# A long convolution with a gated MLP: second rows transposed by a DMA, eleven up products copied out by ScalarE, the first units fed tile by tile, and a new order of tasks

## The chip, the cores and the metric

The kernel runs on one core of a Trainium2 chip. The metric is the device time of one execution in microseconds (us). Shown for the kernel before are the median of three runs and one profiled execution with its trace. Engines are named as in the profile: PE (TensorE matmul), PEld (its weight loads), DVE (VectorE), ACT (ScalarE), POOL (GpSimd) and SP (SyncE, which here only issues DMAs).

## The reference, cut to what matters

The sequence has S = 2048 rows, the model D = 512 columns, the MLP Df = 1792. `A_q` is the row input x; all inputs and the output are bf16.

```python
def _A_ref(q, k, v, shift_k, ssm_k, ssm_D):
    ...
    for t in range(ks):
        k_shift = k_shift + k_pad[:, t:t + S, :] * shift_k[:, ks - 1 - t][None, None, :]
    kv = k_shift * v
    L = 2 * S
    ...
    y_f = kv_f * kf_f[None, :, :, :]
    y = irfft2(y_f, s=(1, L)).astype(jnp.bfloat16)[:, 0, :S, :]
    y = y + kv * ssm_D[None, None, :]
    return q * y

def _B_ref(x, w_gate, w_up, w_down):
    g = jnp.einsum("bsd,df->bsf", x, w_gate)
    u = jnp.einsum("bsd,df->bsf", x, w_up)
    h = _gelu(g) * u
    return jnp.einsum("bsf,fd->bsd", h, w_down)

x = A_q
xn = _layernorm(x, axis=-1)
s = _A_ref(xn, A_k, A_v, A_shift_k, A_ssm_k, A_ssm_D)
g = _silu(_B_ref(xn, B_w_gate, B_w_up, B_w_down))
return x + s * g
```

So there are two independent halves that meet at the end: a causal convolution of length 2048 along the rows (by transforms of length 4096), and a gated MLP on the normalised rows.

## The kernel before, in words

**Layernorm and transposition.** The rows are 16 tiles of 128. Statistics (L837, L838), variance (L848), the power -1/2 on GpSimd (L850) and the normalisation (L858 on ACT, L859 on DVE) make XN from X. The MLP works on row groups q = 0 to 3 of four tiles. For each the transposed rows, xnT, are needed as an operand; xnT has two buffers, used by q in turn. In `xn_transpose` the groups q = 0 and 1 are transposed on PE (L880, four transposes for each tile) and brought from PSUM to xnT by ACT (L621) or DVE (L624); the groups q = 2 and 3 are transposed by one DMA each, issued by SP (L872).

**Units.** A unit (q, m) is one group of 512 rows against one chunk m (0 to 13) of 128 MLP columns: four gate matmuls and four up matmuls (L630, one for each 128 columns of D), a gelu of the gate on ACT into GE (L1183, three buffers), and on DVE the product of GE with the up result, read from PSUM, into HT (L1186). The first two units of q = 0 (`N_HALF`) are cut into two halves of 256 rows, each with its own gelu and product (L1174, L1176). After the units of a group come its `down` matmuls: for each row tile 14 matmuls over the chunks (L630, HT and Wd), then a tanh and a product into G (L1210, L1212), or for the last group a silu, the product with XN and the addition of X (L1218, L1220, L1221). The last row tile is cut into 384 and 128 columns.

**The convolution.** The kernel taps Hn are transposed on PE (L904) into HTr. Stage 1 (`stage1`) then runs on the taps ("H", L946) and on the product of the shifted k with v ("K", L938; the shift is L995 to L1003 on DVE). It has eight units for each. An H unit is four matmuls of 64 rows, two evictions of 1024 columns by ACT (L621) into a slot, an addition on DVE (L955), and a store of the slot to DRAM (`ZH`, 512 KB, a DMA on the ACT queue). The H slots are four, and lie in the late halves of X and XN, which the trace therefore names as the destination; a slot can be taken again only when its store has landed, and the late rows of x can be loaded there only after that. The K units store to `ZK` on the SP queue. Later stages read ZH and ZK back (L1018 and others), multiply the spectra (L1121), go back by way of `ZI`, and give y (L1256), from which the output is formed (L1265 to L1285).

**The order.** Every task (some matmuls, one eviction, one DMA) is added to a list `S` with its possible engines and its estimated cost. `SEQ` is one sequence of task numbers that was found before by a search; a number with a `b` takes the task's second engine. `Sched.run` walks `SEQ`, assigns pool buffers and emits the tasks in that order, so each engine gets its instructions in a fixed order, and a recording layer puts in the semaphore waits. Each engine and each DMA queue works in order: what stands behind a waiting instruction waits too. The planner's costs don't change a kernel by themselves; they decide how buffers are handed out, and were what the search for `SEQ` used. PSUM has eight banks, shared by units, stage 1 and the rest.

**Loads.** All the loads stand on the SP queue in the order of `ORDER`: x, the taps, the weights in chunks, k and v last. Behind the last load of v (SP's row of two V loads at 34.42) come the small transposes of tables (L1029) and the `ZK` stores.

Of the kernel before, what the change touches and what calls it, by code (L numbers as in the profile page):

```python
# [6 lines left out]
BF16 = mybir.dt.bfloat16  # L7
# [46 lines left out]
NC_PAIRS = 4  # L54
SMALL = 1.15 * 262144
T_FWD = 219.0
N_HALF = 2


class Res:  # L60
# [345 lines left out]
def build_kernel(nc, A_q, A_k, A_v, A_shift_k, A_ssm_k, A_ssm_D, B_w_gate, B_w_up, B_w_down, out):  # L406
    with ExitStack() as es0:
# [39 lines left out]
        Drow = new("Drow", [1, DM], BF16)  # L447
        xnT_at = place["at"] + 4096
        xnT = new("xnT", [128, 2, 4, KD, 128], BF16)
        GE = new("GE", [128, 3, 512], BF16)  # L450
        ast_at = place["at"]
        AST = new("AST", [128, 2, 2, 2, DM], BF16)
        g_at = place["at"]
# [889 lines left out]
```

## Time and profile before

| what | value |
|---|---|
| median of three runs | 191.09 us (190.99 to 191.48) |
| the profiled execution, its time | 190.94 us |
| the profiled execution, its span | 189.1 us |
| ACT's share of the span | 72% |
| transposes of XN on PE | 32, of 128 columns each |
| DMA issues of the ZH stores | 8 of 512 KB, all from the ACT queue |

The span runs from the first instruction to the last that the profile shows; 1.84 us of the execution's own time lie around it. A line of the profile reads: source line, engine, operation, destination and source by the program's names, partitions x elements, type, how many, then busy time, mean time of one, and the idle time of the engine just before with what ended it. A timeline line begins with start and length in us; a matmul's end is modelled, so for a run of matmuls the distance between starts is its price. In a DMA issue the last number is the time from the issue to the landing. Names such as "X" and "XN" stand also for the stage-1 slots in their late halves.

### The profile page before, as it was taken

The numbers are of one execution on the slowest core, as the hardware profiler recorded it, in microseconds if no ns is written. First come the engines' busy times: TensorE is split into PE (matmuls) and PEld (weight loads), VectorE is DVE, ScalarE is ACT, GpSimd is POOL, SyncE is SP. The second block draws the span as 40 slices with busy tenths as digits, with TensorE's granted clock in tenths as the row PEclk, the third lists the DMA queues.
The fourth block names the chain that finished last, engine by engine and source line by source line (L and its number), as shares of the span: only waits on it lengthen the run. The fifth ranks groups of instructions, "written<-read, shape, count | busy, mean of one in ns | idle before, by whom it ended". The sixth has DMA issues, their size and how long they took to land.

```text
span 189.1 us, 3534 instructions
## 1 busy us (share of the span) xinstructions
PE 183.5 (97%) x1386; PEld 78.4 (41%) x1386; DVE 168.4 (89%) x250; ACT 136.1 (72%) x185; POOL 12.7 (7%) x26
## 2 busy tenths in 40 slices
PE   7889999999999999999999999999999999999993
PEld 2566344343344333334443433433343444443442
DVE  6979999999999999997499988989999994569994
ACT  6388988996766877876867699887997851253651
POOL 5310920000000000022000000000000000000000
PEclk9999999999999999999999999999999999999999
DMA  5999999999769668289997763999523353967335
GB/s 178 326 382 337 339 373 373 401 414 275 304 239 272 208 227 334 111 243 327 224 310 231 245 206 104 392 284 372 188 112 114 111 170 100 386 208 244 110 142 198
DMA packets 36422, 47.84 MB, mean 253 GB/s; under 512 B 7347, under 2 KB 26039, under 8 KB 36406
## 3 DMA queue, kind: packets, MB, share of 16 engines
q1 hardware_dynamic: 29878, 39.23, 63.7%
q10 hardware_dynamic: 6528, 8.39, 12.5%
q8 instruction: 11, 0.18, 0.4%
q14 instruction: 5, 0.04, 0.1%
HBM read 27.39 MB, written 14.68 MB: 222 GB/s over the span
## 4 chain that ended last, share of the span: by engine, by line
PE 92%; DVE 3%; ACT 2%; POOL 1%; issue 0%
PE psall L630 78%; PE psall L1018 6%; PE psall L946 2%; PE psall L938 2%; PE psall L1256 2%; PE psall L904 2%; POOL mv L850 1%; PE psall L880 1%; ACT L737 1%; DVE stats L837 1%; DVE XN L859 0%; DVE G L1221 0%; DVE G L1220 0%; DVE C L709 0%; ACT G L1218 0%
## 5 line engine op out<-in xcount | busy, mean ns | idle before, releaser
L630 PE MATMUL psall<-xnT,Wu 128*128 128x512 bf16 (+1 forms) x232 | 56.2, 372 | 0.0
L630 PE MATMUL psall<-xnT,Wg 128*128 128x512 bf16 (+1 forms) x232 | 55.3, 372 | 0.5 <-DVE xnT L624 0.5
L630 PE MATMUL psall<-Wd,HT 128*128 128x512 bf16 (+2 forms) x238 | 51.6, 367 | 0.0
L1186 DVE TENSOR_TENSOR HT<-psall,GE 128x512 bf16<-128x512 f32 x54 | 36.1, 680 | 6.5 <-PE psall L630 6.2
L1183 ACT ACTIVATE GE<-psall 128x512 bf16<-128x512 f32 x54 | 31.4, 600 | 12.9 <-PE psall L630 11.6
L630 PEld LDWEIGHTS psall<-Wd,HT 128*128 128x128 bf16 x238 | 21.7, 98 | 27.0 <-issue 3.6
L630 PEld LDWEIGHTS psall<-xnT,Wg 128*128 128x128 bf16 x232 | 21.1, 98 | 27.9 <-issue 3.6
L630 PEld LDWEIGHTS psall<-xnT,Wu 128*128 128x128 bf16 x232 | 21.6, 98 | 26.4 <-issue 2.3
L621 ACT ACTIVATE BO<-psall 128x1024 bf16<-128x1024 f32 x19 | 19.0, 1023 | 7.7 <-PE psall L1018 4.0
L1121 DVE TENSOR_TENSOR HSW<-KB,HSW 128x2048 bf16<-128x2048 bf16 x16 | 19.3, 1220 | 0.3 <-ACT KB L621 0.2
L621 ACT ACTIVATE HSW<-psall 128x1024 bf16<-128x1024 f32 x16 | 15.8, 1031 | 3.5 <-PE psall L1018 3.5
L621 ACT ACTIVATE KB<-psall 128x1024 bf16<-128x1024 f32 x14 | 13.9, 1022 | 2.1 <-PE psall L1018 1.9
L999 DVE TENSOR_TENSOR KTM<-KK,SKB 128x2048 bf16<-128x2048 bf16 x12 | 14.5, 1208 | 0.1
L1001 DVE TENSOR_TENSOR KAC<-KAC,KTM 128x2048 bf16<-128x2048 bf16 x12 | 14.5, 1207 | 0.1
L621 ACT ACTIVATE AST<-psall 128x1024 bf16<-128x1024 f32 x12 | 12.3, 1023 | 1.4 <-PE psall L938 1.2
L1210 ACT ACTIVATE G<-psall 128x512 bf16<-128x512 f32 x12 | 7.2, 601 | 7.8 <-PE psall L630 6.8
L850 POOL TENSOR_TENSOR mv<-mv,NHALF 128x1 f32<-128x1 f32 (+1 forms) x7 | 7.1, 1021 | 67.4 <-DVE mv L848 64.7
L837 DVE BATCH_NORM_STATS2 stats<-X 128x6 f32<-128x512 bf16 x16 | 10.8, 683 | 0.8 <-DMA X<-in_A_q_dram 0.8
L1121 DVE TENSOR_TENSOR KB<-KB,HSW 128x2048 bf16<-128x2048 bf16 x8 | 9.6, 1222 | 0.1
L1144 DVE TENSOR_TENSOR HSW<-HSW 128x2048 bf16<-128x2048 bf16 x8 | 9.7, 1218 | 0.0
L621 ACT ACTIVATE X<-psall 128x1024 bf16<-128x1024 f32 x8 | 8.2, 1023 | 1.0 <-PE psall L946 0.9
L621 ACT ACTIVATE XN<-psall 128x1024 bf16<-128x1024 f32 x8 | 8.1, 1024 | 1.0 <-PE psall L946 0.9
(85 smaller groups left out, 152.3 us busy)
## 6 DMA issues: line engine op xcount, KB each, us to landing
BH<-ZH SPq DMA_DIRECT2D x8, 512.0 KB, 4.4
BK<-ZK SPq DMA_DIRECT2D x8, 512.0 KB, 6.3
HSW<-HSW SPq DMA_DIRECT2D x16, 256.0 KB, 3.5
ZI<-BO ACTq DMA_DIRECT2D x16, 256.0 KB, 3.0
BI<-ZI SPq DMA_DIRECT2D x8, 512.0 KB, 4.7
ZK<-AST SPq DMA_DIRECT2D x6, 512.0 KB, 3.1
Hn<-in_A_ssm_k_dram SPq DMA_DIRECT2D x4, 512.0 KB, 7.4
KK<-in_A_k_dram SPq DMA_DIRECT2D x4, 512.0 KB, 11.2
```

The lines of the kernel that those rows point to most:

```text
L621: return h.activation(o, i, ACTF.Copy, scale=scale)
L630: return h.matmul(o, lhsT=l, rhs=r, start=st, stop=sp)
L837: t_stats[t] = op([("DVE", 670.0)], lambda e, h, t=t: h.bn_stats(stats[:, t, :], X[:, t, :]), r=[bX[q][t % 4]], w=[bst[t]], rr=[R_X[t]], w ...
L850: t_pw = op([("POOL", 2500.0 if q else 600.0)], lambda e, hd, ts=ts, n=n: hd.tensor_tensor(mv[:, ts, 3:4], mv[:, ts, 2:3], NHALF[:, 0:n, : ...
L999: op([("DVE", dur)], lambda e, h, j=j, m=m: h.tensor_tensor(KTM[:, m.slot, :, :], kk(j), sk(j), ALU.mult), r=need + [bSKB[j], a], w=[m], r ...
L1001: op([("DVE", dur)], lambda e, h, m=m: h.tensor_tensor(KAC[:, a.slot, :, :], KAC[:, a.slot, :, :], KTM[:, m.slot, :, :], ALU.add), r=[m], ...
L1018: trk.op("PE", lambda h: h.matmul(ps(s, i)[b, :], lhsT=wt(col)[a, :], rhs=data(col)[a, :], start=n < 16, stop=n >= len(todo) - 16, tile_po ...
L1121: return hd.tensor_tensor(pair(KB, *(2 * DM * z for z in slots())) if to else x, k, x, ALU.mult)
L1144: return hd.tensor_tensor(x, x, y, ALU.add)
L1183: op([("ACT", act(512))], lambda e, h: h.activation(GE[:, g.slot, :], bank(pg), ACTF.Gelu_apprx_tanh), r=[pg], w=[g], rr=lambda: R_bank(pg ...
L1186: op([("DVE", dve(512, 1))], lambda e, h: h.tensor_tensor(HT[:, q % 2, m, :], bank(pu), GE[:, g.slot, :], ALU.mult), r=[pu, g], w=[bHT[q][m]],
L1210: op([("ACT", act(n))], lambda e, h, g=g, pc=pc: h.activation(g, pc(), ACTF.Tanh, scale=0.5), r=[p], w=[bt], rr=lambda p=p: R_bank(p), ww= ...
```

## The change

The change has five parts.

1. `xn_transpose`: the second row group (q = 1) is transposed by a DMA on SP too, without a condition on earlier units. Its 16 PE transposes and four evictions go.
2. `UNITS`: for 11 units, (0, 6), (0, 8), (0, 10), (0, 12) and (1, 0) to (1, 12) with even m, the up result is first copied from PSUM into a new bf16 buffer `U_` of two slots, and the product is taken from there. In the built program all eleven copies stand on ACT.
3. The first two units of q = 0: the gate and up matmuls go by single row tiles (64 matmuls of 128 columns in the place of 32 of 256). Their gelus and products stay as they were.
4. The variance of the layernorm (`var`) takes the transform table `F1` as a further input of its task; and the planner's costs for the SP queue's DMAs are others (a transposition's 6700 becomes 4300, its landing is computed anew).
5. `SEQ` is a new sequence. Seen on the engines: the eight H units of stage 1 stand ahead of the first unit of q = 1, as do 42 of the 56 down matmuls of q = 0 (before: seven H units and nine down matmuls). On ACT the first four ZH stores stand in one group behind the last gelus of q = 0, and the four others follow one by one. The last y group (L1256) has 38 down matmuls behind it where it had 42. The four evictions of xnT of q = 0 are on ACT (two were on DVE). In the first microseconds the sine table and its load come later on ACT and the iotas for the identities earlier on GpSimd. The new DMA stands on SP behind the last load of v and ahead of the small transposes.

```diff
@@ -25,27 +25,28 @@
 SEQ = (
-    "2 3 16 0 7 17 18 19 20 21 1 10 8 22 9 11 23 24 25 65 66 12 4 6 48 67 26 5 73b 49 68 76 74 75 86 90 77 78 87 71 91b 27 28 29 30 72 82 83 69 70 "
...
+    "16 17 18 19 2 4 6 3 0 20 21 7 10 11 22 1 8 9 23 24 25 65 66 5 73b 67 12 68 76 74 75 77 69 49 86 90 48 78 361 26 70 27 79b 28 87 349 91 71 351 72 "
...
 )
@@ -55,6 +56,7 @@
 N_HALF = 2
+UNITS = [(0, 6), (0, 8), (0, 10), (0, 12), (1, 0), (1, 2), (1, 4), (1, 6), (1, 8), (1, 10), (1, 12)]
@@ -372,7 +374,13 @@
-                if en < self.EARLY:
+                if eng == "SP":
+                    pipe = max(pipe, t.start + 780.0, max(l.end for l in order if l.eng == "loads") - 760.0) + t.nbytes / self.DMA_BW
+                    t.end = pipe + 760.0
+                    if t.nbytes > 750000.0 and t.start < 52000.0:
+                        t.end = max(t.end, t.start + 9700.0)
+                        pipe = t.end - 760.0
+                elif en < self.EARLY:
@@ -448,6 +456,7 @@
+        U_ = new("U_", [128, 2, 512], BF16)
@@ -537,6 +546,7 @@
+        R_U = [res(f"U{j}", U_[:, j, :]) for j in range(2)]
@@ -575,6 +585,7 @@
+        pU = Pool_("U", 2)
@@ -846,7 +857,7 @@
-                t_var = op([("DVE", 180.0)] + ([] if q else [("ACT", 240.0)]), var, r=[bconst, *bm], w=[be], rr=rm + [R_ep], ww=rm)
+                t_var = op([("DVE", 180.0)] + ([] if q else [("ACT", 240.0)]), var, r=[bconst, bF1, *bm], w=[be], rr=rm + [R_ep], ww=rm)
@@ -866,11 +877,11 @@
         def xn_transpose(q):
-            if q > 1:
+            if q > 0:
...
-                S.add([("SP", 6700.0)], f, r=bXN[4 * q:4 * q + 4], w=bxnT[q], nbytes=W_XT, after=gu_tasks[q - 2])
+                S.add([("SP", 4300.0)], f, r=bXN[4 * q:4 * q + 4], w=bxnT[q], nbytes=W_XT, after=gu_tasks[q - 2] if q > 1 else [])
                 return
@@ -1170,7 +1181,8 @@
                     for p, W, nm in ((p2[0], Wg, "g"), (p2[1], Wu, "u")):
-                        gu_tasks[q].append(S.add([("PE", pe(4, 256))], half(p, W, nm, 2 * i, 2 * i + 2), r=[bW[nm][ci], *bxnT[q][2 * i:2 * i + 2]], w=[p], lat=150.0))
+                        for j in (2 * i, 2 * i + 1):
+                            gu_tasks[q].append(S.add([("PE", pe(4, 128))], half(p, W, nm, j, j + 1), r=[bW[nm][ci], bxnT[q][j]], w=[p], lat=150.0))
@@ -1183,6 +1195,12 @@
             af = (down_tasks[q - 2] if q >= 2 else []) + (s1_tasks["H"] if q == 1 else [])
+            if (q, m) in UNITS:
+                ub = B(f"ub{q}_{m}", pU)
+                op(EV(512), lambda e, h: copy(e, h, U_[:, ub.slot, :], bank(pu)), r=[pu], w=[ub], rr=lambda: R_bank(pu), ww=lambda: [R_U[ub.slot]])
+                op([("DVE", dve(512, 2))], lambda e, h: h.tensor_tensor(HT[:, q % 2, m, :], U_[:, ub.slot, :], GE[:, g.slot, :], ALU.mult), r=[ub, g], w=[bHT[q][m]],
+                   rr=lambda: [R_U[ub.slot], R_GE[g.slot]], ww=[R_HT[q % 2][m]], after=af)
+                return
             op([("DVE", dve(512, 1))], lambda e, h: h.tensor_tensor(HT[:, q % 2, m, :], bank(pu), GE[:, g.slot, :], ALU.mult), r=[pu, g], w=[bHT[q][m]],
```

41 rows, old and new, of the table SEQ are left out of this document.

## The prediction

> **What bounds the kernel now.** I read the page's busy row and its chain of waits first, then a table of busy time by stretch, cut where the kernel changes its work.
>
> ```profile
> span 189.1 us, 3534 instructions
> PE 183.5 (97%) x1386; PEld 78.4 (41%) x1386; DVE 168.4 (89%) x250; ACT 136.1 (72%) x185; POOL 12.7 (7%) x26
> PE 92%; DVE 3%; ACT 2%; POOL 1%; issue 0%
> ```
> ```profile
> 5.55:12.18 6.63, 5.33 (x49) 4.20 (x50) 5.27 (x16) 2.84 (x6) 2.56 (x4) 1.00 1.05 352
> 25.00:43.84 18.84, 18.84 (x106) 7.95 (x103) 18.84 (x24) 16.95 (x25) 0.00 (x0) 1.00 1.06 389
> 43.84:80.00 36.16, 36.16 (x179) 14.08 (x178) 35.84 (x42) 27.63 (x35) 0.00 (x0) 1.00 0.76 243
> ```
> The columns of the last fence are the stretch and its length, the busy time of PE, PEld, DVE, ACT and POOL with the number of instructions, PE's granted clock, the DMA share and GB/s. PE holds 92% of the chain, is busy for the whole of the two long stretches, and has the full clock (1.00). So time can be gained by removing PE work or the idle time of the head, and any new PE wait is paid in full. DVE (35.84 of 36.16) is as full as PE from 43.84 to 80; until 43.84 the DMA share is above 1, so transfers are scarce.
>
> **PE work removed and added.** The PE timeline gives the price of each matmul by its start-to-start time.
>
> ```profile
> 8.15 1.05 PE L630 MATMUL psall<-xnT,Wg 128*128 128x256 bf16 x8 [0.53 <-DVE xnT L624]
> 14.78 0.60 PE L630 MATMUL psall<-xnT,Wu 128*128 128x256 bf16 x4
> 15.21 1.03 PE L630 MATMUL psall<-xnT,Wg 128*128 128x512 bf16 x4
> 16.08 1.03 PE L630 MATMUL psall<-xnT,Wu 128*128 128x512 bf16 x4
> 32.17 0.39 PE L880 MATMUL psall<-ident,XN 128*128 128x128 bf16 x4
> 32.40 1.03 PE L630 MATMUL psall<-xnT,Wu 128*128 128x512 bf16 x4
> 40.59 0.83 PE L880 MATMUL psall<-ident,XN 128*128 128x128 bf16 x12
> 41.26 2.11 PE L630 MATMUL psall<-Wd,HT 128*128 128x512 bf16 x9
> 43.30 0.61 PE L946 MATMUL psall<-HTr,F 64*128 64x512 bf16 x4
> 43.84 1.90 PE L630 MATMUL psall<-xnT,Wg 128*128 128x512 bf16 x8
> ```
> Four matmuls of 512 columns take 16.08 − 15.21 = 0.87, 0.216 each; of 256 columns 0.43, 0.108 each; a stage-1 group of four 43.84 − 43.30 = 0.54. The 16 transposes of the second rows (q = 1) take 0.23 (32.17 to 32.40) and 0.67 (40.59 to 41.26): **−0.90**, 0.056 each, all on PE's path.
>
> The first two units exchange 32 matmuls of 256 columns (32 × 0.108 = 3.46) for 64 of 128. No row shows 128 moving columns of this product back to back in the head; the nearest is the transpose, also 128 × 128 in bf16: 64 × 0.056 = 3.58. **+0.10** to one digit (bounds 0 and the 2.8 of rival D).
>
> The weight loads' row bears on that.
>
> ```profile
> L630 PEld LDWEIGHTS psall<-xnT,Wu 128*128 128x128 bf16 x232 | 21.6, 98 | 26.4 <-issue 2.3
> ```
> The Trainium skill, "TensorE: Matmul & The Clock Gate", section "Back-to-back issue gap", speaks against this part: it puts sustained N = 128 at about 81 ns with the weight loads, not the 56 ns of a matmul alone. By it the pieces would be 64 × 81 ns = 5.2, 1.7 more than now (an estimate). The trace disagrees for the transposes, which load a weight each too and stand 0.056 apart.
>
> What the pieces buy is the head. In 5.55 to 12.18 stand 16 transposes of Hn, 16 of XN and 16 matmuls of 256 columns; at 0.119 (the next row: eight from 11.23 to 12.18, an upper bound), 0.056 and 0.108 that is 4.5 of 6.63, so 2.1 is idle. A piece needs only its own row tile, so it can start before the 0.53 wait at 8.15 is over; but the weights must have landed.
>
> ```profile
> 11.23 1.11 PE L904 MATMUL psall<-ident,Hn 128*128 128x128 f32 x8
> 2.11 0.43 SPq L603 DMA_DIRECT2D Wg<-in_B_w_gate_dram  x1
> Wg<-in_B_w_gate_dram SPq DMA_DIRECT2D x1, 256.0 KB, 5.7
> ```
> Wg lands at 2.11 + 5.7 = 7.8, 0.35 before the 8.15 of now. So the gain is about **−0.30**. Bounds: −0.7 if the later pieces also fill the waits at the third and fourth tile; +0.5 if they come later, because all four evictions of q = 0 now stand on ScalarE where two stood on DVE, or because the variance now waits for F: behind it stand the power on GpSimd and the normalised rows, and for those PE's transposes. The sine table, the phases and the iotas change places in the same 7 us; ACT has 3.8 of 6.63 free here, so I take 0 for them, within the same bounds.
>
> **Copies of the up products.** An eviction of 11 products moves from a DVE product that reads PSUM to an ACT copy and a product out of SBUF.
>
> ```profile
> L1186 DVE TENSOR_TENSOR HT<-psall,GE 128x512 bf16<-128x512 f32 x54 | 36.1, 680 | 6.5 <-PE psall L630 6.2
> L1220 DVE TENSOR_TENSOR G<-G,XN 128x512 bf16<-128x512 bf16 x3 | 1.3, 423 | 0.0
> L621 ACT ACTIVATE xnT<-psall 128x512 bf16<-128x512 bf16 x6 | 3.3, 598 | 1.6 <-PE psall L880 1.6
> ```
> DVE: 11 × (680 − 423) ns = −2.8. ACT: 11 × 0.60 = +6.6, less the four evictions of q = 1 (2.4). Four copies fall before 43.84, where they replace those evictions (ACT stays at 17 of 18.84); seven fall in 43.84 to 80, where ACT goes from 27.6 to 31.8 of 36.16. Both lie beside PE: **0**, DVE having 1.8 more room where it has least. Uncovered, a copy would cost its 0.60 when PE wants that bank: bounds 0 and 11 × 0.60, the latter only if every bank were short; I take 0 since no stretch fills ACT.
>
> **The tail.** After the last y group 38 matmuls stand where there were 42; the four of 384 columns moved ahead take 4 × 0.162 (384/512 of 0.216) = 0.65 of cover for the last DVE chain, which now has 0.49 to spare.
>
> ```profile
> 185.94 0.36 DVE L1220 TENSOR_TENSOR G<-G,XN 128x384 bf16<-128x384 bf16 x1 [0.49 <-ACT G L1218]
> ```
> That is 0 to +0.16; I take **+0.05**. PE sum: −0.90 + 0.10 − 0.30 + 0.05 = **−1.05**.
>
> **The DMA for the second rows.** It goes on SP behind the last V load, ahead of the MI and G1 transposes and of ZK. The new order puts the first unit of q = 1 later: after all 42 down matmuls and all eight H groups it has ahead (33 more matmuls and one group than now). Need: 43.84 + 33 × 0.216 + 0.54 − 0.90 + 0.10 − 0.30 = 50.4. Landing:
>
> ```profile
> 34.42 0.91 SPq L603 DMA_DIRECT2D V<-in_A_v_dram  x2
> 35.37 2.29 SPq L1029 DMA_TRANSPOSE MI<-TFA  x1
> 38.98 0.84 ACT L858 ACTIVATE XN<-X,NB__69,mv 128x512 bf16<-128x512 bf16 x1
> V<-in_A_v_dram SPq DMA_DIRECT2D x1, 512.0 KB, 11.2
> MI<-TFA SPq DMA_TRANSPOSE x1, 11.2
> 87.04 1.18 SPq L603 DMA_DIRECT2D HSW<-HSW  x2
> HSW<-HSW SPq DMA_DIRECT2D x2, 256.0 KB, 5.2
> 88.31 4.25 SPq L872 DMA_TRANSPOSE xnT<-XN  x1
> xnT<-XN SPq DMA_TRANSPOSE x1, 6.3
> ```
> The last V load (issued at 34.9) lands at 46.1. Three ZH stores (26.56, 28.00, 28.40) now share the engines with it; the new order issues none before all of unit q = 0, so 3 × 512 KB at 389 GB/s, 1.35 each, leave its way: 42.1. The transposition of the third rows landed at 88.31 + 6.3 = 94.6, 1.9 behind the transfer ahead (second HSW, issued at 87.5, +5.2 = 92.7): so 44.0, or about 49.4 if four ZH stores (5.4) get in between. Both are before 50.4: hidden, **0**; uncovered it costs what it lands late (rival B).
>
> **The new wait.** In the new order four ZH stores stand together on the ACT queue, behind the last gelu of q = 0. An H stage-1 slot is free only when its store has landed, and the eviction behind them (X from PSUM, 1.02) waits for the first.
>
> ```profile
> 26.56 0.38 ACTq L603 DMA_DIRECT2D ZH<-XN  x1
> 28.40 0.52 ACTq L603 DMA_DIRECT2D ZH<-XN  x1
> 43.95 0.37 ACTq L603 DMA_DIRECT2D ZH<-X  x1
> ZH<-XN ACTq DMA_DIRECT2D x1, 512.0 KB, 7.1
> ZH<-X ACTq DMA_DIRECT2D x1, 512.0 KB, 3.9
> ZH<-XN ACTq DMA_DIRECT2D x1, 512.0 KB, 2.8
> 48.25 2.08 ACT L621 ACTIVATE X<-psall 128x1024 bf16<-128x1024 f32 x2 [0.92 <-PE psall L946]
> ```
> PE ends q = 0 now at 40.59, with six H groups done and four of the transposes; the new order has four groups: 40.59 − 2 × 0.54 − 0.23 + 0.10 − 0.30 = 39.1. The last gelus wait for buffers that DVE's products free, so I put the stores one gelu (0.60) and an issue behind PE, at 39.8. PE then has 9 down matmuls, the fifth group, 14 down matmuls, and reaches the sixth group at 39.1 + 23 × 0.216 + 0.54 = 44.6, which needs the bank that the waiting eviction frees. So the store must land by 44.6 − 1.02 = 43.6. Alone a store takes 2.8: 42.6. Behind the transfers already queued it takes longer (7.1 at 26.56): the store of 43.95 landed at 47.8, 1.7 behind the last V load and 1.2 behind MI (35.4 + 11.2 = 46.6), both issued before it. Here that gives 42.1 + 1.7 = 43.8 behind V alone, 44.0 + 1.2 = 45.2 behind the transposition of q = 1, 46.2 with MI on top. I take 45.2, the row being one of a store behind a transposition: the eviction ends at 46.2, PE waits 46.2 − 44.6 = **+1.6** (bounds 0 and 2.6). What is behind it on ACT, the tanh of the first down product and three more evictions, comes late with it; so do groups seven and eight and with them the first unit of q = 1, which PE does not get back.
>
> Sum: −1.05 + 1.6 = +0.55 on the span of 189.1; with 1.84 around it the profiled execution goes from 190.94 to 191.5. The median shown (191.09) is 0.15 above that execution: **191.6**.
>
> **Rivals.** A, the stores share the engines at once. At half of 389 GB/s 512 KB take 2.7 plus the 1.5 that a store alone has beyond its bytes (2.8 − 1.35): 39.8 + 4.2 = 44.0, a wait of 0 to 0.4, −1.05 to −0.65: 190.0 to 190.4, **faster**. Against it: the store of 26.56 should then have taken 4.2, and took 7.1. For it: the 3.9 of the store of 43.95. The Trainium skill, "DMA: Bandwidth & Descriptors", section "Queues, rings and completion order", says that an engine goes round between its queues packet by packet, which is this rival; the 7.1 disagrees, as no store should wait for another queue's backlog.
>
> B, the transposition lands after its need. The layernorm of its last row tile now ends at 38.98 + 0.84 = 39.8; the new order has it ahead of the last gelus of q = 0, but if it comes as late as now and the transposition takes MI's 11.2, it lands at 51.0, and with all four stores in between (5.4) at 56.4. At the middle, 53.7, the first unit of q = 1 waits 3.3, with the store's wait inside it: −1.05 + 3.3, 193.3, **slower**. It decides from 51.5 on, where the wait passes the gain. Against it: the 6.3 of the third rows, and a layernorm that is put earlier.
>
> C, the gain is given back before 43.84 without any store's wait: DVE is busy for all of 25.00 to 43.84, so a product of q = 0 that comes one product and one copy (0.68 + 0.60) late stops the down matmuls behind it: −1.05 + 1.28 = +0.2, 191.3, **same**. For it: DVE's 18.84 of 18.84; against it: the four copies take 4 × 0.26 off that.
>
> D, the pieces go at the pace of their weight loads: 64 × 98 ns = 6.27, +2.8 over 3.46; with −0.90, −0.30 and 0.05 that is +1.65 and no store's wait: 192.7, **slower**. Against it: 56 ns.
>
> **How the numbers follow.** A difference under 0.3% (0.57) can't be told from none. Forecast 0.50 (190.0 to 192.8 by its own bounds: 0.34 slower, 0.14 the same, 0.02 faster), A 0.26 (faster), B 0.12 and D 0.04 (slower), C 0.08 (0.06 same, 0.02 slower). Faster 0.28, same 0.20, slower 0.52. The range goes from 190.0, A's full gain, to 193.2, which leaves out the upper half of B.
>
> **What would show it.** Right: PE's first wait of over 1 us between 44 and 47, released by ACT's X eviction, that eviction ending its own wait on a ZH store that took 4.5 to 6.5; 56 ns per piece; xnT landed by 50; no PE wait at the first unit of q = 1. Wrong: stores of under 4.5 (A), a PE wait on xnT's DMA near 50 (B), pieces 98 ns apart (D), or a PE wait of a microsecond before 40 or after 55.

## The result, and the profile after

| | before | after |
|---|---|---|
| median | 191.04 us (190.98 to 191.48) | 197.56 us (195.66 to 199.40) |
| ratio to before, 95% interval | | 1.0239 [1.0213, 1.0266] |
| the profiled execution, its time and span | 190.94, 189.1 | 195.66, 193.8 |

The median of after lies between two executions at 195.7 and two at 199.3 to 199.4; the latter had a lower mean clock (0.983 and 0.973 against 0.991 and 0.989) and are left out of the ratio, as such executions are out of every ratio below, while the medians are of all. By the ratio the change makes the kernel 4.6 us slower. The forecast was 191.6, in a range of 190.0 to 193.2.

The page of after, its busy row and its chain of waits:

```profile
span 193.8 us, 3565 instructions
PE 185.4 (96%) x1402; PEld 79.3 (41%) x1402; DVE 165.5 (85%) x246; ACT 141.5 (73%) x196; POOL 12.6 (7%) x26
...
PE 73%; DMA 9%; DVE 8%; SPq 4%; ACT 3%; POOL 2%; issue 1%; DVEq 0%
```

PE's share of the chain fell from 92% to 73%, and a DMA stands in it with 9%. These shares are not times lost: the store of ZH is 4% of the span, and the rest of the DMA's share, and SP's 4%, belong to the load of shift_k and the issues ahead of it in the first 19 us, through which the chain now reaches that store. PE is busy 1.9 us longer than before although it has less to do, which points to matmuls at a lower clock. Where is told by the table by stretch (stretch and length, busy PE, PEld, DVE, ACT and POOL, PE's granted clock, DMA share, GB/s):

```profile
43.84:60.00 16.16, 13.42 (x58) 4.62 (x57) 12.17 (x15) 11.00 (x14) 0.00 (x0) 0.89 0.79 253
60.00:80.00 20.00, 20.00 (x100) 7.68 (x97) 19.64 (x23) 18.14 (x26) 0.00 (x0) 1.00 0.77 255
```

Before, PE was busy for all of 43.84 to 80 at the full clock. Now 2.7 us are idle between 43.84 and 60 and the clock there is 0.89; from 60 on PE is full again. PE's timeline through that stretch:

```profile
39.53 2.11 PE L641 MATMUL psall<-Wd,HT 128*128 128x512 bf16 x9
41.57 0.61 PE L957 MATMUL psall<-HTr,F 64*128 64x512 bf16 x4
...
45.23 0.39 PE L957 MATMUL psall<-HTr,F 64*128 64x512 bf16 x1
48.36 0.60 PE L957 MATMUL psall<-HTr,F 64*128 64x512 bf16 x3 [2.74 <-ACT X L632]
48.90 3.78 PE L641 MATMUL psall<-Wd,HT 128*128 128x512 bf16 x9
52.61 0.60 PE L957 MATMUL psall<-HTr,F 64*128 64x512 bf16 x4
53.15 2.33 PE L641 MATMUL psall<-Wd,HT 128*128 128x512 bf16 x10
...
55.95 1.04 PE L641 MATMUL psall<-xnT,Wg 128*128 128x512 bf16 x4
```

The sixth H group starts at 45.23 and goes on at 48.36: less the 0.13 that one of its matmuls takes (0.54 / 4), a pause of 3.0 us, released by ACT's eviction of X. Behind it stands what no step of the prediction had: nine down matmuls take 52.61 − 48.90 = 3.71, where the nine from 39.53 take 2.04. They ran at about half the clock, and lost 1.7. The ten from 53.15 have the full clock again. ACT's and SP's timelines and the DMA issues say what the eviction waited for:

```profile
40.23 0.92 ACTq L614 DMA_DIRECT2D ZH<-X  x2
...
47.28 3.00 ACT L632 ACTIVATE X<-psall 128x1024 bf16<-128x1024 f32 x3 [3.29 <-DMA ZH<-X]
```
```profile
37.44 5.20 SPq L883 DMA_TRANSPOSE xnT<-XN  x1
42.69 1.32 SPq L1040 DMA_TRANSPOSE MI<-TFA  x1
```
```profile
ZH<-X ACTq DMA_DIRECT2D x1, 512.0 KB, 7.0
xnT<-XN SPq DMA_TRANSPOSE x1, 10.8
```

The first store is issued at 40.23 and lands 7.0 later, at 47.2; the eviction starts at 47.28. Ahead of it on SP stood the new transposition, and MI's behind that. The transposition itself landed at 37.44 + 10.8 = 48.2, long before its first reader at 55.95. The packets that moved while the store waited, in the microsecond from 41 to 42 and in that from 44 to 45 (queue 1 is SP's, queue 10 ACT's; a queue's row has packets, MB and the share of the engines' time):

```profile
DMA packets 122, 0.08 MB, mean 80 GB/s; under 512 B 109, under 2 KB 109, under 8 KB 122
...
q1 hardware_dynamic: 122, 0.08, 52.2%
```
```profile
DMA packets 61, 0.09 MB, mean 86 GB/s; under 512 B 22, under 2 KB 22, under 8 KB 61
...
q10 hardware_dynamic: 39, 0.08, 87.2%
```

The loads, at 400 GB/s until 40, are over. From 41 to 42 the engines move 80 GB/s, nearly all in packets of under 512 B, which are the transposition's; not one packet of the queued stores moves. From 44 to 45 the stores' packets occupy 87% of the engines' time and still move no more than 0.08 MB. So it is not the number of bytes that is in the stores' way. The store's 7.0 has two parts: none of its packets moves until 43.6, while the transposition's do, and from 44 to 46 packets of both queues are slow (86 and 225 GB/s). With nothing transposed ahead the first packet of a store moves 0.7 to 0.9 after its issue (in the kernel with the transposition behind the stores, below).

The kernel before had such a microsecond too, from 45 to 46, behind MI's transposition and with stores queued:

```profile
DMA packets 135, 0.07 MB, mean 67 GB/s; under 512 B 121, under 2 KB 121, under 8 KB 135
...
q1 hardware_dynamic: 126, 0.05, 34.4%
q10 hardware_dynamic: 9, 0.02, 13.3%
```

It costs nothing there: PE is busy throughout. The prediction read only the landing times of that store, not this rate.

### The profile page after: what moved, and what is told of

It reads as the page before. It is cut to its first block, busy times and chain, and to the rows that moved or that the text cites. A ratio compares the mean times of both kernels' runs of the same rounds, so it can differ in the third digit from the quotient of the medians.

```text
span 193.8 us, 3565 instructions
## 1 busy us (share of the span) xinstructions
PE 185.4 (96%) x1402; PEld 79.3 (41%) x1402; DVE 165.5 (85%) x246; ACT 141.5 (73%) x196; POOL 12.6 (7%) x26
## 4 chain that ended last, share of the span: by engine, by line
PE 73%; DMA 9%; DVE 8%; SPq 4%; ACT 3%; POOL 2%; issue 1%; DVEq 0%
PE psall L641 62%; DMA SKR<-in_A_shift_k_dram 6%; PE psall L1029 5%; DMA ZH<-X 4%; SPq L614 4%; PE psall L949 2%; PE psall L1274 2%; ACT X L632 2%; POOL SKB L987 2%; PE psall L957 1%; DVE KAC L1012 1%; DVE G L1239 1%; DVE G L1238 1%; DVE XN L1291 1%; DVE HT L1204 1%
## 5 line engine op out<-in xcount | busy, mean ns | idle before, releaser
L641 PE MATMUL psall<-xnT,Wg 128*128 128x512 bf16 (+1 forms) x248 | 56.3, 359 | 0.4 <-ACT xnT L632 0.3
L641 PE MATMUL psall<-Wd,HT 128*128 128x512 bf16 (+2 forms) x238 | 54.3, 376 | 0.0
L641 PEld LDWEIGHTS psall<-xnT,Wu 128*128 128x128 bf16 x248 | 22.3, 98 | 27.1 <-issue 3.3
L641 PEld LDWEIGHTS psall<-xnT,Wg 128*128 128x128 bf16 x248 | 21.7, 98 | 27.4 <-issue 3.1
L1204 DVE TENSOR_TENSOR HT<-psall,GE 128x512 bf16<-128x512 f32 x43 | 28.4, 681 | 4.4 <-PE psall L641 3.5
L632 ACT ACTIVATE BO<-psall 128x1024 bf16<-128x1024 f32 x20 | 19.9, 1024 | 9.8 <-PE psall L1274 5.3
L1230 DVE SCALAR_TENSOR_TENSOR G<-G,psall 128x512 bf16<-128x512 bf16 x12 | 8.1, 681 | 5.5 <-ACT G L1228 5.5
## 6 DMA issues: line engine op xcount, KB each, us to landing
KK<-in_A_k_dram SPq DMA_DIRECT2D x4, 512.0 KB, 11.1
```

Source lines behind the costliest of these rows:

```text
L632: return h.activation(o, i, ACTF.Copy, scale=scale)
L641: return h.matmul(o, lhsT=l, rhs=r, start=st, stop=sp)
L1204: op([("DVE", dve(512, 1))], lambda e, h: h.tensor_tensor(HT[:, q % 2, m, :], bank(pu), GE[:, g.slot, :], ALU.mult), r=[pu, g], w=[bHT[q][m]],
L1230: op([("DVE", dve(512, 1))], lambda e, h, g=g, pc=pc: h.scalar_tensor_tensor(out=g, in0=g, scalar=1.0, in1=pc(), op0=ALU.add, op1=ALU.mult ...
```

## The experiments

Each is the changed kernel with one edit, unless said otherwise. "Pause" is PE's wait inside an H group as above, "store" the time of the first ZH store from issue to landing; both are from the profiled execution. The ratio is to the kernel before on the same chip.

| kernel | median us | ratio [95%] | pause | store |
|---|---|---|---|---|
| after | 197.56 | 1.0239 [1.0213, 1.0266] | 3.0 | 7.0 |
| pause filled, 14 matmuls | 194.44 | 1.0158 [1.0132, 1.0183] | 0.5 + fill | |
| pause filled, 4 matmuls | 193.52 | 1.0084 [1.0028, 1.0139] | none | 3.4 |
| transposition behind the stores | 190.48 | 0.9963 [0.9948, 0.9978] | none | 4.2 |
| three stores earlier | 191.21 | 0.9990 [0.9967, 1.0013] | 1.4 | 10.2 |
| q = 1 transposed on PE | 193.75 | 1.0139 [1.0090, 1.0188] | 1.9, fifth group | 4.7 |
| the same, three stores earlier | 192.89 | 1.0074 [1.0040, 1.0108] | 1.4 | 11.1 |
| plain copy for the transposition | 193.34 | 1.0081 [1.0046, 1.0116] | 3.5 | 7.5 |
| plain copy, MI's transposition late | 191.65 | 1.0025 [1.0006, 1.0044] | 1.0 | 5.0 |
| MI's transposition late | 198.60, lowest 196.28 | none on record | 5.6 | 9.6 |
| before, with the DMA alone | 200.54 | 1.0469 [1.0446, 1.0493] | 6.0, at q = 1 | |
| transposition late, no copies | 193.47 | 1.0113 [1.0094, 1.0133] | 0.7, twice | |
| transposition late, pieces of 256 | 191.20 | 0.9995 [0.9982, 1.0009] | | |
| transposition late, old tail | 190.28 | 0.9960 [0.9945, 0.9976] | | |

### Is the second loss the clock's?

Fourteen products of 512 columns, whose result the group then overwrites, are put on PE ahead of the sixth H group, where it would wait.

```diff
+FILL_U, FILL_N = 5, 14
...
+                    if u == FILL_U:
+                        for _ in range(FILL_N):
+                            trk.op("PE", lambda h: h.matmul(ps(psl(pp[0]), 0), lhsT=Wd[:, 0, 0:128], rhs=HT[:, 0, 0, :], start=True, stop=True),
+                                   r=[R_HT[0][0], R_Wd[0]], w=[R_ps[psl(pp[0])][0]], accum=True)
```

> The changed kernel with 14 matmuls of 512 columns put ahead of the sixth H group, into a bank that the group overwrites, so that they run while PE waits for the ScalarE eviction behind the first ZH store (their results are not used). Theory (the store costs a wait of 3.0 us, and PE standing idle for it costs 1.7 us more, as the nine down matmuls behind the wait then go at half the clock): the eviction still ends near 48.3, the nine down matmuls take 1.9 to 2.1 us in place of 3.7, the granted clock is 1.00 from 43.84 to 60, and the time is 195.7 - 1.7 = 194.0 us. Rival (the clock falls for another reason, such as the transposition by DMA or the work before): the clock falls all the same and the time stays at 195.7, or more by what the 14 matmuls add.

PE's timeline of that kernel:

```profile
48.77 0.60 PE L962 MATMUL psall<-HTr,F 64*128 64x512 bf16 x3 [0.26 <-ACT X L633]
49.30 2.12 PE L642 MATMUL psall<-Wd,HT 128*128 128x512 bf16 x8
51.35 0.61 PE L962 MATMUL psall<-HTr,F 64*128 64x512 bf16 x4
```

The group goes on at 48.77, as late as without the fill, but the down matmuls behind it take 51.35 − 49.30 = 2.05, the full clock. With more work on PE the kernel is 1.3 us faster than after's 195.7. That the slow matmuls hang on PE standing idle is shown for this pause; that an idle PE always brings them is not (a pause of 3.5 below brought none). The pause of 3.0 itself is the larger part and stays.

With four of them (`FILL_N = 4`) the question was how short a pause still costs the clock.

> As fill_the_wait with 4 matmuls in place of 14 (0.9 us), so that PE pauses some 2.2 us at the sixth group in place of 3.1. Theory (a pause of 2 us or more halves the clock for the next eight or nine matmuls of 512 columns, as behind the 2.0 us of second_rows_on_pe, and 1.5 us, as in stores_early, don't): the nine down matmuls behind the pause take 3.7 us, the clock falls below 1.00 in 43.84 to 60, and the time is that of the changed kernel, 195.7 us, since the four matmuls fill time that was idle. Rival (it takes about 3 us): the nine take 2.0 us, the clock stays, and the time is 194.0.

This one gave no answer at its place. In the profiled execution a load of Hn came late and the whole order after it; the stores, issued at 42.84, took 3.4 and PE had no pause at the sixth group. What it showed lies elsewhere: that late load stopped PE for 2.1 us at 19.00, and the four matmuls of 512 columns behind it took 0.44 each instead of 0.216; the granted clock was 0.50 from 21 to 23. Two more executions took 192.4 and 192.5, less than either expectation (195.7 and 194.0); they have no trace, so why stays open.

### Is it the transposition that keeps the stores?

The DMA for q = 1 is made to wait for the first ZH store, so that it is queued behind the stores instead of ahead of them. MI's transposition, which stands behind it on SP, goes out later with it (47.94 in place of 42.69); everything else stays.

```diff
-r=R_XN[4 * q:4 * q + 4], w=R_xnT[q % 2])
+r=R_XN[4 * q:4 * q + 4] + ([R_Z["H"][7]] if q == 1 else []), w=R_xnT[q % 2])
```

> The changed kernel with the DMA of the second rows made to wait until the first ZH store has landed; no instruction changes its place on any engine. Theory: the store lands 2.8 to 3.5 us after its issue (43 to 43.8), PE doesn't wait at the sixth group and the clock stays; the transposition is issued near 43.5 and lands at 50 if it takes 6.3 as for the third rows, up to 54 if it takes 10.8 as now, against a need at 51.3: 191.0 to 193.8 us. Rival (the loads of v hold the store): the store still lands after 46, the transposition lands after 52, and the time is above 196 us.

The timelines of PE, ACT and SP, the DMA issues, and the packets from 42 to 43 us:

```profile
44.40 1.01 PE L957 MATMUL psall<-HTr,F 64*128 64x512 bf16 x4
45.34 2.12 PE L641 MATMUL psall<-Wd,HT 128*128 128x512 bf16 x9
...
50.73 1.04 PE L641 MATMUL psall<-xnT,Wg 128*128 128x512 bf16 x4
```
```profile
39.46 0.97 ACTq L614 DMA_DIRECT2D ZH<-X  x2
43.73 3.00 ACT L632 ACTIVATE X<-psall 128x1024 bf16<-128x1024 f32 x3
```
```profile
43.72 4.17 SPq L883 DMA_TRANSPOSE xnT<-XN  x1
```
```profile
xnT<-XN SPq DMA_TRANSPOSE x1, 5.8
```
```profile
DMA packets 189, 0.38 MB, mean 381 GB/s; under 512 B 3, under 2 KB 3, under 8 KB 189
```

The first store goes out at 39.46, and at 43.73 the eviction behind it runs: 4.2 us. The engines move 381 GB/s where after's rows have 80 and 86. The sixth group has no pause, the clock stays, and the first unit of q = 1 is at 50.73 instead of 55.95. Although the transposition starts 6.3 us later than in after, it lands only 1.3 later (49.5), before its need. One dependency is worth 5.2 us, and the kernel is 0.4% faster than before. Which of the two transpositions had been in the way this run can't say.

The other way round, three of the four first stores go out earlier, ahead of the transposition (three numbers of `SEQ` moved up).

> The changed kernel with three of the four ZH stores taken out of their group and issued as soon as their slots are complete (behind the normalised rows of q = 1 on ScalarE, ahead of the last gelus of q = 0), the fourth left where it was. Theory (the wait comes from where the stores stand behind the transposition, not from their number): the first store, issued near 36.5, lands near 43.6 as the store of 26.56 did before (7.1 us behind queued loads), PE doesn't wait at the sixth group, the clock stays, and the time is 195.7 - 4.7 = 191.0 us, up to 192 if the transposition, now behind three stores, lands after the first unit of q = 1 needs it. Rival (a store is held until the loads and the transposition are both through, whenever it is issued): it lands at 46 to 47, and the time stays above 195.

PE's timeline of that kernel:

```profile
44.90 0.39 PE L957 MATMUL psall<-HTr,F 64*128 64x512 bf16 x1
46.41 0.60 PE L957 MATMUL psall<-HTr,F 64*128 64x512 bf16 x3 [1.12 <-ACT X L632]
```

The pause shrinks to 1.4 and the clock holds behind it (the next nine matmuls take 2.05). But the first store, issued at 35.09, took 10.2 and landed at 45.3: it was queued while loads still ran, and from 37.11 on the transposition was beside it. An issue 5.1 earlier than in after brought a landing 1.9 earlier. Neither expected landing (near 43.6, or 46 to 47) came; the median of 191.21 lies near the expected 191.0, although the profiled execution (192.04) has a pause of 1.4 that this sum didn't have; whether the others have it isn't known.

Then the second rows go back to PE (`if q > 1:` in `xn_transpose`, with a `SEQ` that has the 16 transposes and their evictions in it), so that no large transposition is there.

> The changed kernel with the second rows transposed on PE again (16 transposes behind the last unit of q = 0, evicted by ScalarE behind the four ZH stores) and no DMA for them; all else in the new order. Theory (the first ZH store is held by the transposition that stands in the DMA engines when it is issued): the first store lands 2.8 to 3.5 us after its issue, near 43.5 to 44, PE doesn't wait at the sixth group, the clock stays at 1.00, and the time is 195.7 - 3.0 - 1.7 + 0.9 = 191.9 us. Rival (the loads of v still queued hold the store, whatever the transposition): the store takes 6 to 7 us, PE waits 2 us or more, and the time is 195 to 197 us.

PE's timeline and ACT's:

```profile
41.95 0.39 PE L958 MATMUL psall<-HTr,F 64*128 64x512 bf16 x1
43.93 1.09 PE L958 MATMUL psall<-HTr,F 64*128 64x512 bf16 x3 [1.58 <-ACT xnT L633]
44.95 4.61 PE L642 MATMUL psall<-Wd,HT 128*128 128x512 bf16 x14
```
```profile
43.27 2.07 ACT L633 ACTIVATE xnT<-psall 128x512 bf16<-128x512 bf16 x4 [3.49 <-DVE V L1015]
```

The first store takes 4.7, although MI's transposition, issued at 32.45, is ahead of it and the engines move only 79 GB/s from 41 to 42: a transposition ahead does not always hold a store for long. For the total the run says nothing: where the evictions of xnT stand, four store issues occupy ACT until 42.9, and PE waits 1.9 one group earlier. The profiled execution also lost clock (14 matmuls in 49.49 − 44.95 = 4.54, where the 14 of after from 42.11 take 3.12); the three others, at 193.2 to 194.3, have a mean clock of 0.998 or 1.0.

The same with the evictions ahead of the stores and three stores early:

> As stores_early (three ZH stores taken out of their group), with the second rows transposed on PE and no DMA for them; their four evictions stand on ScalarE ahead of the fourth store, so that the fifth H group doesn't wait for them behind four store issues as it did in second_rows_on_pe. Theory (without the transposition in the DMA engines the stores land in time, PE doesn't pause, and the 16 transposes cost their 0.9 us): 190.5, as transposition_late, + 0.9 = 191.4 us, and stores that take 4 to 7.5 us. Rival (the stores are late without the transposition too): a PE wait of over 1 us at the sixth group and 192.5 or more.

It missed what it was made for. The first store, issued at 35.19, took 11.1, with no transposition of rows anywhere, and PE paused 1.4 at the sixth group. What did stand ahead was MI's transposition of tables (SP, 33.12). That raised the question of the next three.

### A transposition or its bytes, and which one?

The DMA for q = 1 becomes a plain copy of the same 512 KB, so the rows of q = 1 are not transposed.

```diff
+                    if q == 1:
+                        trk.dma("SP", lambda h: h.dma_start(out=xnT[:, 1, :, :, :].rearrange("k j d p -> k (j d p)"), in_=XN[:, 4:8, :].rearrange("p t d -> p (t d)")), d_xt, r=R_XN[4:8], w=R_xnT[1])
+                        return
```

> The changed kernel with a plain DMA copy of the same 512 KB in the place of the transposition of the second rows, so that xnT of q = 1 holds rows that aren't transposed. Theory (it is the transposition's way of holding the engines that keeps the store back, with the engines nearly idle from 41 to 42.6): the first store takes 4.2, as without anything ahead, plus at most 1.35 for the copy's bytes, 4.2 to 5.6; PE waits 0.2 to 1.6 us, the clock stays, and the time is 190.7 to 192.2 us. Rival (any 512 KB ahead of the store does the same): the store takes 7 us and the time is 195.7.

The store still took 7.5 and PE paused 3.5. But SP had issued the copy in 0.54, and MI's transposition now went out at 37.39, again ahead of the stores. So MI's was held back behind the first store, once with the copy and once with the transposition for q = 1:

```diff
-                trk.dma(e, lambda h: h.dma_start(out=out_ap, in_=in_ap, transpose=True), d_g1, r=[rr], w=[ww])
+                trk.dma(e, lambda h: h.dma_start(out=out_ap, in_=in_ap, transpose=True), d_g1, r=[rr, R_Z["H"][7]], w=[ww])
```

> As plain_copy (a plain copy of 512 KB in place of the transposition of the second rows, so xnT of q = 1 holds rows that aren't transposed), with the small transposition MI from TFA, which stood right behind that copy and ahead of the stores in plain_copy, made to wait until the first ZH store has landed. Theory (any transposition that the stores meet in the DMA engines holds them, MI too; a copy's bytes don't): with none ahead, the first store takes 4.2 to 5.6 us, the engines don't fall to 0.1 MB per us, PE waits at most 1.5 us, and the time is 190.5 to 192 us. Rival (512 KB ahead of the store hold it, transposed or not): the store takes 7 to 8 us and the time is 192.5 or more, as in plain_copy.

> The changed kernel with only the small transposition MI from TFA held until the first ZH store has landed; the transposition of the second rows stands where the change put it, ahead of the stores. Theory (the transposition of the second rows holds the stores by itself): the first store takes 6.5 us or more, PE waits 2.5 us or more at the sixth group, and the time is 194 to 195.7 us (the latter with the clock's loss). Rival (it is MI alone, which transposition_late held back as well because it stands behind the other on SP): the store takes 4 to 5.6, and the time is 190.5 to 192.

First the kernel with the plain copy: PE's timeline, the DMA issues, the packets from 42 to 43 us.

```profile
45.23 0.39 PE L960 MATMUL psall<-HTr,F 64*128 64x512 bf16 x1
46.41 0.60 PE L960 MATMUL psall<-HTr,F 64*128 64x512 bf16 x3 [0.79 <-ACT X L632]
```
```profile
ZH<-X ACTq DMA_DIRECT2D x1, 512.0 KB, 5.0
```
```profile
DMA packets 187, 0.40 MB, mean 397 GB/s; under 512 B 15, under 2 KB 15, under 8 KB 187
```

Then the one with the transposition: PE's timeline, and the packets from 44 to 45 us.

```profile
44.72 0.39 PE L957 MATMUL psall<-HTr,F 64*128 64x512 bf16 x1
50.42 1.03 PE L957 MATMUL psall<-HTr,F 64*128 64x512 bf16 x3 [5.32 <-ACT X L632]
```
```profile
DMA packets 185, 0.07 MB, mean 74 GB/s; under 512 B 170, under 2 KB 170, under 8 KB 185
```

The two differ only in whether the 512 KB for q = 1 are transposed. Copied, the engines keep 397 GB/s, the store takes 5.0 (0.8 more than with nothing ahead, within the 1.35 that the copy's bytes take) and the pause is 1.0. Transposed, they fall to 74 GB/s, the store takes 9.6 and the pause is 5.6. So it is the transposition and not its bytes. Each of the two on SP held the store without the other: MI's alone for 7.5 (the first plain copy), that of q = 1 alone for 9.6, though MI's issued at 32.45 did not (4.7, above). The time of the last kernel, 197.50 in the profiled execution and 196.28 at the lowest, is above the 194 to 195.7 that was expected: its pause is 2.6 longer than after's, for which no run gives the reason.

### What the parts are worth

These start from the kernel with the transposition behind the stores, at 190.48. First without the eleven copies (`UNITS = []`; each product stands in `SEQ` where both its inputs are there):

> The kernel transposition_late (second rows' DMA behind the first ZH store) without the eleven copies: each product reads the up result from PSUM, in the place where both its inputs stand in the order. Theory (the copies cost nothing where they stand, and give DVE 2.8 us of room in a stretch, 43.84 to 60, that DVE fills wholly even with them): DVE holds PE up, and the time is 1 to 3 us above transposition_late, 191.5 to 193.5. Rival (the copies bring nothing, as DVE's fullness is waiting work and not the bound): within 0.3 us of 190.5.

PE's timeline, and a row of the table by stretch:

```profile
45.83 0.60 PE L957 MATMUL psall<-HTr,F 64*128 64x512 bf16 x3 [0.41 <-ACT X L632]
...
52.56 0.60 PE L641 MATMUL psall<-xnT,Wg 128*128 128x512 bf16 x2
```
```profile
60.00:80.00 20.00, 19.22 (x94) 7.16 (x94) 19.74 (x23) 16.09 (x21) 0.00 (x0) 1.00 0.76 246
```

It loses 3.0. The sixth and the seventh group wait 0.7 each (the row at 45.83 is the sixth's), the first unit of q = 1 is 1.8 later (52.56), and in 60 to 80 PE has 0.8 idle, with DVE full (19.74 of 20). So the copies do more than cost nothing: in this order, which was made with them, PE loses 3.0 without them. With DVE that full, it is the likely bound; the two pauses end on ACT's eviction of X.

Then with pieces of 256 columns as before in place of the single row tiles, in the same places of the order:

> The kernel transposition_late with the first two units by halves of 256 rows again, as before the change. Theory (the pieces buy about 0.3 us of the head and cost 0.1): 0.2 us more, 190.6 to 190.9. Rival (the pieces are paced by their weight loads and cost 1.6 or more): 189 or less; second rival (the head gains 0.7 by them): 191.2.

The kernel is back at 191.20, 0.7 later; the intervals lie just apart (0.9978 and 0.9982). Its first piece waits until 8.99 for a pair of tiles, where the single tile started at 7.73.

Last, the four matmuls of 384 columns go back behind the last y group:

> The kernel transposition_late with the four matmuls of 384 columns that the new order had moved ahead put back behind the last y group, as before the change; nothing else moves. Theory (they are the cover of the last DVE chain, and the tail behind PE's last matmul is 0.2 to 0.25 us longer without them): 0.2 us less, 190.2 to 190.3. Rival (the tail is set by the last row tile's own chain, whatever stands ahead of it): 190.5, no change.

190.28 against 190.48, with intervals that lie on each other: the tail can't be told from nothing. These two are the fastest versions here, below both kernels.

### The DMA in the old order

The kernel before, with its order and only `if q > 0:` in `xn_transpose`, the 16 transposes and their evictions dropped from `SEQ`:

> The kernel before with one part of the change alone: the second rows transposed by a DMA on SP behind the last load of v, in the order of before. Theory (a transposition issued behind the last normalised row, at 39.8, lands 5.8 to 10.8 us later, and the old order wants it at 43.8 - 0.9 = 42.9): PE waits 2.7 to 7.7 us at the first unit of q = 1, and the clock falls behind a wait of 2 us or more (+1.7): 191.1 - 0.9 + 2.7 + 1.7 = 194.6 to 199.6 us. Rival (the transposition is hidden in any order): 190.2.

PE's timeline of that kernel:

```profile
44.20 0.61 PE L947 MATMUL psall<-HTr,F 64*128 64x512 bf16 x4
50.77 3.57 PE L631 MATMUL psall<-xnT,Wg 128*128 128x512 bf16 x8 [5.97 <-DMA xnT<-XN]
54.13 1.66 PE L631 MATMUL psall<-Wd,HT 128*128 128x512 bf16 x5
```

PE waits 6.0 for xnT and then has eight matmuls in 54.13 − 50.77 = 3.36, for 1.73 at the full clock. Here the wait is rival B's, at the place where the new order avoids it: the later first unit of q = 1 belongs to this DMA. The time, 199.91 at the lowest, is above the expected 194.6 to 199.6.

## Why the prediction was wrong, point by point

**The direction and the mechanism were right.** PE's first long wait stands inside the sixth H group, is released by ACT's X eviction, and that waits for a ZH store. The group was reached at 45.2, for 44.6 forecast. No PE wait stands at the first unit of q = 1, and the transposition landed before 50, though at 48.2 and not at 44.0.

**The step that failed is the new wait, +1.6 with bounds of 0 and 2.6: it was 3.0, and took 1.7 more of clock with it.** The landing of the store was set at 5.4 after its issue, 1.2 behind a transposition put at 44.0. The store took 7.0 and the transposition landed at 48.2. The step treated what is queued ahead as bytes and a delay of one landing; the runs show a store of 4.2 with nothing transposed ahead, 5.0 behind the same bytes copied, and 7.0, 7.5 and 9.6 with a transposition in front (4.7 and 3.4 in two kernels, see Open). The upper bound, MI's transposition on top, was 0.4 short, and its reason isn't borne out: with MI's held back the wait was 5.6.

**A term was missing.** The sum priced a pause by its length alone. Nine matmuls at half the clock behind it make +1.7, as large as the whole wait that was forecast. The filled pause shows that here it hangs on PE's idleness.

**Sizes.** The first down matmul was at 39.53 instead of 39.1; since the same order has it at 38.91 in the kernel with the late transposition, that 0.4 is within what executions differ by. The four H groups up to 55.95 cost 0.64 and not 0.54 each, with 0.1 for the change of tile shape beside them: before's own row has it (nine down matmuls from 41.26 to 43.30 are 2.04, and 9 × 0.216 is 1.94). The first unit of q = 1 stood at 55.95 instead of 50.4 + 1.6 = 52.0; 0.4 + 1.4 + 1.7 + 0.4 = 3.9 of those 3.95 are told. The tail cost +0.24 (last matmul to the end: 3.18, before 2.94), for 0.05 forecast and 0.16 as its bound.

**What held.** The pieces stand 0.056 apart, twelve from 22.82 to 23.49 in after's timeline of PE:

```profile
22.82 0.83 PE L641 MATMUL psall<-xnT,Wu 128*128 128x128 bf16 x12
23.49 0.39 PE L641 MATMUL psall<-xnT,Wg 128*128 128x128 bf16 x4
```

So rival D is out. With what the pieces cost (0.10) and brought (−0.30) the prediction had −0.2; taking them away costs 0.7, so that with a cost of 0.10 the head gained 0.8, just beyond its bound (−0.7). The copies cost nothing, as said, but the cover they give, 3.0 in this order, was not seen. Rival A's time, 190.0 to 190.4, is near that of the kernel with the transposition late (190.48). There the change without the new wait is worth 0.7 (0.37% of 191.28) for the 1.05 of the sum; since the pieces alone are worth 0.7, that the sum comes near is in part luck. Rival A failed on its condition, engines shared at once. The Trainium skill, "DMA: Bandwidth & Descriptors", section "Queues, rings and completion order", says that engines go round between queues by packet. Once packets of both queues move the trace agrees: from 33 to 34 us in before queue 1 has 133 packets and queue 10 has 133. What neither rival A nor the sum had as a term is the time until a store's first packet: the store that before issues at 26.56 has none until 30.5, and that which after issues at 40.23 none until 43.6.

**Open.** What starts the slow phase isn't settled. In the kernel with four filling matmuls the stores followed the transposition by 2.5 us and took only 3.4: the slow phase (83 GB/s from 42 to 43) was over before their first packet. In before a store behind MI's took 3.9, with q = 1 on PE 4.7. In every trace with a microsecond under 100 GB/s ahead of the first store's landing, the transposition had been issued while loads still ran. In the kernel with the transposition behind the stores it was issued at 43.72, when they were over and only stores ran, and the engines kept 212 to 220 GB/s from 46 to 49. So the phase may need loads in flight; no run varied that alone. Nor does a run say whether it is the transposition as such or its packets of under 512 B, of which the plain copy has few (15 of 187).

## What to carry to other kernels

A DMA transposition is not a background transfer of so many bytes: put stores that free a buffer ahead of it on the queues, by a dependency if the issue order doesn't do it, and hold small table transpositions back too. Before a landing time is carried over from another transfer, look at the DMA rate of each microsecond around it; the one at 67 GB/s in the trace of before was the warning. Price a PE pause of two microseconds or more at its length plus up to 1.7 of clock, and look whether useful matmuls can stand in it.

## What the runs showed of the hardware

- With a transposition queued ahead, the 16 DMA engines moved 74 to 86 GB/s in the microseconds shown, in which 381 to 397 were moved without one, also while the stores' own packets held 87% of the engines' time.
- Pauses of PE and the matmuls of 512 columns behind them: after 3.0 (+1.7 in nine matmuls), before with the DMA alone 6.0 (+1.6 in eight), MI late 5.6 (nine in 3.12, +1.1), the late load of Hn 2.1 (four at half the clock) and q = 1 on PE 1.9 (14 matmuls +1.4, in one of four executions by their mean clocks). A pause of 1.4 cost no clock; nor did one of 3.5, in PE's timeline of the kernel with the plain copy:

```profile
48.27 0.60 PE L960 MATMUL psall<-HTr,F 64*128 64x512 bf16 x3 [3.28 <-ACT X L632]
48.80 2.12 PE L641 MATMUL psall<-Wd,HT 128*128 128x512 bf16 x9
```

So the length does not decide alone. The Trainium skill, "TensorE: Matmul & The Clock Gate", section "HAM oscillation — how this bites in real kernels", gives the rule of no PE-idle gaps over about 3.4 us; here 1.9, 2.1 and 3.0 sufficed and 3.5 did not. Its section "What's actually happening" has the activity judged in a free-running window, which would explain the spread (no run here shows it), and the way back after about 3.4 us of work; the 3.7 of the nine slow matmuls agrees with the latter.
